# Decay tables of a long convolution: low factors from ScalarE exponentials instead of GpSimd products, amplitude multiplied in by VectorE, and a new placement of the side work

## The chip, the cores and the metric

One core of a Trainium2 chip runs the whole program. Its engines are TensorE (PE, with PEld for its weight loads), VectorE (DVE), ScalarE (ACT), GpSimd (POOL), and SyncE (SP), which here only issues transfers. Each engine works through its own list of instructions in the order written, and waits on semaphores of the others. The metric is the device time of one execution in microseconds (us); lower is better.

## The reference, cut to what matters

```python
h = layernorm(x) * (1 + ca) + sa                 # x: 2048 x 640; sa..gb from silu(c) @ w_mod
P = exp(dt * (A_re + 1j*A_im) * l)               # 640 channels x 192 states x 2048 steps
K = einsum("dn,dnl,dn->dl", C, P, dt * B).real   # a 2048-step filter for each channel
x = x + ga * (causal_conv(h, K) + h * Dskip)     # by FFT in the reference
h = layernorm(x) * (1 + cb) + sb
x = x + gb * (((h @ w_gate) * (h @ w_up)) @ w_down)   # 640 -> 1536 -> 640
```

## The kernel before, in words

The channels are taken in 5 blocks of 128 (`db`). Each block makes 8 groups (`n`, 40 in all), and each half block of 4 groups (`hf` = 0 to 9) has its own set of small tables. A group needs for its share of (channel, state) rows a decay `exp(a*l)` and a phase. The 2048 steps are split in two factors of a product, so that a matrix product over the states (`kg_ma`, `kg_mb`) gives the filter: `P` holds 32 values and `Q` 64 values a row, and both are a magnitude (`EP`, `EQ`) times a cosine or sine.

The magnitudes are outer products made by GpSimd in `outer` (line 716): `EP` from a low table `LP` (8 steps of 64) and a high table in `RH`; `EQ` from a low table `LQ` (8 consecutive steps, with the amplitude of the state in it) and a high table in `RH`. The phases `Ph` are integer outer sums of `LH` and `DH`, made on the same line. For every group GpSimd issues one `Ph`, one `EQ` and one `EP`. ScalarE then takes sines (`trig`), VectorE multiplies them with `EP` and `EQ` into `PtA`, `PtB`, `QtA`, `QtB` (lines 771, 772, 777, 797), and TensorE multiplies those.

The small tables of a block come from `u_seeds(db)`, a generator that is advanced a segment at a time; a letter string (`SEG`) says which steps (`s_l`, `s_a`, ...) a segment holds. Its core is a run on ScalarE of square root, exponentials (`s_e`), arctangent, with a load of a function table between kinds; after it the phase start `psi` goes through TensorE and VectorE to GpSimd (`weighted`). Before, `s_e` makes for each half the seven nontrivial columns of `LP` by seven exponentials of 96 elements, exponentiates `RH`, and exponentiates `RL`, three powers that `tab_eq` on GpSimd doubles into `LQ`: a copy of the amplitude, a product, and two doublings. `tab_ph` on GpSimd makes `LH` from `DL`, of which there are two buffers, one for each half; VectorE fills `DL` and `DH` in `s_d`.

The order around this is written out by a table. The main loop has 144 steps `t`, three to a group, and 24 more after the last group. At each step two calls of `due` issue the side jobs that fall into it. `SCHED` gives for each job the moment of each of its segments, 20 units to a step `t`, so 2400 is the end of the 40 groups; negative numbers fall into the prologue. The side jobs are the layernorm statistics (`st`, `hm`, `rstd`), the modulation rows (`ml`, `mr`, `mc`, `fo`), the seeds of the next block (`q`), the low tables (`low`), and the stages of the convolution: `pre` (first transform of h), `g`, `k` (transform of the filter), `c` (product and back), `d` (last stage and residual). The letters in `SLOT` give the ring buffer that each allocation takes. After the loop the gated product (the rest of the program) runs with an order of its own.

Of the kernel before, what the change touches and what calls it, by code (L numbers as in the profile page):

```python
# [31 lines left out]
    ml=(-885, -929, -989),  # L32
    mr=(((98, 154), (90, 130)), ((-884, 78), (-877, 73)), ((-885, -881), (-889, 132))),
    st=(
        (-955, 11),
        (-929, 195),
        (-874, 149),
        (-925, 128),
        (-938, 121),
        (-879, 152),  # L40
        (-869, 167),
        (-924, 162),
        (-995, -925),
        (-938, -871),
        (-885, 93),
        (-990, -871),
        (50, 180),
        (51, 214),
        (-930, -878),
        (-927, 39),  # L50
    ),
    hm=(
        (120, 388),
        (119, 390),
        (123, 234),
        (-949, 306),
        (-1000, 254),
        (112, 246),
        (231, 293),
        (-871, 309),  # L60
        (266, 333),
        (324, 384),
        (315, 372),
        (134, 256),
        (463, 511),
        (335, 429),
        (391, 541),
        (479, 545),
    ),
    rstd=(228, 229),  # L70
    tab=(487, 829),
    fo=(157, 189, 197, 222),
    e0=(138,),
    ds=(250, 255, 397, 411),
    mc=((-872, 289, 307, 356, 356), (217, 378, 439, 446, 461), (309, 570, 620)),
    q=(
# [4 lines left out]
    ),  # L81
    pre=(
# [5 lines left out]
    ),  # L88
    c=(
# [5 lines left out]
    ),  # L95
    d=(
# [5 lines left out]
    ),  # L102
    k=(
        (189, 202),
        (208, 226),
        (356, 358),
        (499, 559),
        (422, 496),
        (634, 660),
        (663, 672),  # L110
        (698, 713),
        (672, 682),
        (820, 837),
        (947, 972),
        (1036, 1059),
        (915, 955),
        (956, 984),
        (1080, 1094),
        (1072, 1079),
        (1271, 1275),  # L120
        (1209, 1209),
        (1528, 1540),
        (1546, 1546),
        (1406, 1429),
        (1384, 1393),
        (1533, 1569),
        (1521, 1521),
        (1684, 1715),
        (1706, 1716),
        (1931, 1933),  # L130
        (1939, 1951),
        (1911, 1915),
        (2069, 2083),
        (2033, 2056),
        (1997, 2004),
        (2286, 2306),
        (2108, 2128),
        (2368, 2376),
        (2349, 2373),
        (2504, 2534),  # L140
        (2413, 2437),
        (2492, 2495),
        (2495, 2507),
    ),
    low=((145, 411, 641, 885, 1122, 1398, 1592, 1847, 2073), (209, 434, 680, 929, 1150, 1398, 1612, 1868, 2112)),
    w=(2508, 2575, 2790, 2776, 2819, 2829),
    wl=(2444, 2450),
    wm=(2801, 2834),
    h=(2480, 2716, 2875, 2876, 2878, 2878, 2878, 2878),
    g=(  # L150
# [1716 lines left out]
```

## Time and profile before

| what | value |
|---|---|
| time, median of 3 runs | 983.3 us (982.86 to 986.79) |
| span of the profiled execution | 985.5 us |
| PE busy in it | 892.4 us (91%) |
| DVE busy | 717.3 us (73%) |
| ACT busy | 579.4 us (59%) |
| POOL busy | 513.1 us (52%) |
| last `EP` on POOL begins | 435.6 us |

The profile gives one execution, whose span from the first to the last instruction is 985.5 us; a time of its own beside that span is not shown, and the runs lie between 982.86 and 986.79 us. The shares of busy time are means over two stages that have little in common: until about 437 us GpSimd makes tables for the 40 groups and all engines share work, after about 531 us the gated product runs with TensorE nearly always busy, and between them lies the tail of the convolution. So the profile is read by stage.

### The profile page before, as it was taken

The numbers are of one execution on the slowest core, as the hardware profiler recorded it, in microseconds if no ns is written. First come the engines' busy times: TensorE is split into PE (matmuls) and PEld (weight loads), VectorE is DVE, ScalarE is ACT, GpSimd is POOL, SyncE is SP. The second block draws the span as 40 slices with busy tenths as digits, with TensorE's granted clock in tenths as the row PEclk, the third lists the DMA queues.
The fourth block names the chain that finished last, engine by engine and source line by source line (L and its number), as shares of the span: only waits on it lengthen the run. The fifth ranks groups of instructions, "written<-read, shape, count | busy, mean of one in ns | idle before, by whom it ended". The sixth has DMA issues, their size and how long they took to land.

```text
span 985.5 us, 26662 instructions
## 1 busy us (share of the span) xinstructions
PE 892.4 (91%) x11134; PEld 725.6 (74%) x11134; DVE 717.3 (73%) x1297; ACT 579.4 (59%) x1076; POOL 513.1 (52%) x400
## 2 busy tenths in 40 slices
PE   4767898899789888999879999999999999999998
PEld 3565656686476667677636888889999788888997
DVE  8798569888978888794867755557676656578952
ACT  4869989986878797873336433334455443435430
POOL 5988899799779979970030254440113132322110
PEclk9977789899989889999999999999999999999999
DMA  7746664555255434658695666733564576758875
GB/s 260 257 151 212 213 198 137 175 174 173 77 154 175 146 114 116 192 166 269 208 257 189 230 202 188 240 110 132 176 224 129 192 234 220 233 168 293 243 239 187
DMA packets 158816, 188.53 MB, mean 191 GB/s; under 512 B 9828, under 2 KB 128360, under 8 KB 157544
## 3 DMA queue, kind: packets, MB, share of 16 engines
q1 hardware_dynamic: 149480, 155.51, 49.1%
q0 software_dynamic: 4752, 21.63, 7.6%
q10 hardware_dynamic: 4464, 9.70, 2.6%
q8 instruction: 87, 1.43, 0.6%
q14 instruction: 33, 0.27, 0.1%
HBM read 124.22 MB, written 62.59 MB: 190 GB/s over the span
## 4 chain that ended last, share of the span: by engine, by line
PE 56%; ACT 14%; DVE 13%; issue 10%; POOL 4%; DMA 3%; SPq 0%; POOLq 0%; ACTq 0%; DVEq 0%
PE pa L1078 18%; PE psg L1078 9%; PE pa L1502 7%; PE kg L812 2%; PE kg L827 2%; PE psfc L894 2%; PE psfb L894 2%; PE psfc L950 2%; ACT trb L230 2%; ACT L230 2%; PE psfa L894 1%; ACT tra L230 1%; DVE QtA L772 1%; DVE QtA L771 1%; PE psfc L873 1%
## 5 line engine op out<-in xcount | busy, mean ns | idle before, releaser
L1055 POOL TENSOR_TENSOR tf<-wur,wgb 128x256 f32<-128x256 f32 x23 | 17.4, 755 | 243.0 <-DVE wtl L1026 196.5
L716 POOL TENSOR_TENSOR EQ<-LQ,RH 128x1536 f32<-128x1536 f32 x40 | 124.2, 3106 | 8.3 <-DVE QtB L772 8.1
L1026 DVE TENSOR_TENSOR wtl<-tf,wth 128x256 fp32r<-128x256 f32 (+1 forms) x72 | 37.3, 520 | 58.6 <-ACT wth L230 58.4
L716 POOL TENSOR_TENSOR Phb<-LH,DH 128x1536 int32<-128x1536 int32 x20 | 62.3, 3114 | 13.2 <-ACT tra L230 13.2
L716 POOL TENSOR_TENSOR EP<-LP,RH 128x768 f32<-128x768 f32 x40 | 66.1, 1653 | 0.0
L716 POOL TENSOR_TENSOR Pha<-LH,DH 128x1536 int32<-128x1536 int32 (+1 forms) x21 | 62.5, 2974 | 1.9 <-ACT trb L230 1.6
L1502 PE MATMUL pa<-wsg,sh 128*128 128x384 f32 (+1 forms) x304 | 57.3, 307 | 0.0
L827 PE MATMUL kg<-QtB,PtB 64*32 64x64 f32 x2560 | 49.3, 232 | 7.1 <-DVE QtB L772 7.1
L827 PEld LDWEIGHTS kg<-QtB,PtB 64*32 64x32 f32 x2560 | 42.8, 117 | 17.1 <-DVE QtB L772 8.5
L1541 POOL DMA_DIRECT2D wsg<-wdc x21 | 11.1, 531 | 66.5 <-PE pa L1554 35.5
L1502 PEld LDWEIGHTS pa<-wsg,sh 128*128 128x128 f32 x304 | 45.1, 188 | 0.0
L1026 DVE TENSOR_TENSOR wsg<-wga,wsg 128x640 fp32r<-128x640 f32 x36 | 33.8, 946 | 13.2 <-ACT wsg L230 13.2
L230 ACT ACTIVATE sh<-a 128x512 fp32r<-128x512 f32 x55 | 33.3, 624 | 13.9 <-PE psg L1554 6.2
L1026 DVE TENSOR_TENSOR sl<-a,sh 128x512 fp32r<-128x512 f32 x55 | 38.0, 710 | 3.9 <-ACT sh L230 3.9
L230 ACT ACTIVATE wsg<-wga 128x640 fp32r<-128x640 f32 x36 | 26.1, 730 | 24.8 <-PE pa L1502 12.1
L1078 PE MATMUL pa<-hh,wsg 128*128 128x512 f32 x150 | 39.9, 392 | 0.0
L771 DVE TENSOR_TENSOR QtA<-tra,EQ 128x1024 f32<-128x1024 f32 x20 | 24.4, 1221 | 18.1 <-PE kg L812 8.7
L1148 POOL TENSOR_SCALAR hfa<-xb,hr,hr 128x128 f32<-128x128 f32 x4 | 2.3, 577 | 67.0 <-DVE hr L285 67.0
L230 ACT ACTIVATE s<-pa 128x512 f32<-128x512 f32 x12 | 7.2, 599 | 49.1 <-PE pa L1078 49.1
L230 ACT ACTIVATE a<-pa 128x512 f32<-128x512 f32 x12 | 7.2, 597 | 48.4 <-PE pa L1078 48.4
L230 ACT ACTIVATE wth<-tf 128x256 fp32r<-128x256 f32 (+1 forms) x72 | 32.5, 482 | 4.6 <-DVE tf L1056 1.8
L1078 PE MATMUL pa<-sh,wth 128*128 128x512 f32 x110 | 34.0, 390 | 0.4 <-ACT a L230 0.4
(640 smaller groups left out, 3125.4 us busy)
## 6 DMA issues: line engine op xcount, KB each, us to landing
wsg<-wdc POOLq DMA_DIRECT2D x21, 640.0 KB, 4.8
wgb<-B_w_gate SPq DMA_DIRECT2D x24, 320.0 KB, 4.7
wur<-B_w_up SPq DMA_DIRECT2D x24, 320.0 KB, 5.7
wsd<-wsg SPq DMA_DIRECT2D x12, 640.0 KB, 4.2
wga<-wdg SPq DMA_DIRECT2D x12, 640.0 KB, 4.0
wsg<-wsd POOLq DMA_DIRECT2D x12, 640.0 KB, 4.9
wdc<-xb SPq DMA_DIRECT2D x21, 320.0 KB, 3.4
TVb<-WD SPq DMA_DIRECT2D x22, 256.0 KB, 3.4
```

The lines of the kernel that those rows point to most:

```text
L230: return S.activation(o, i, f, **kw)
L716: G.tensor_tensor(o.rearrange("p x (h l) -> p x h l", l=8), lo.unsqueeze(2).to_broadcast([P, rows, nh, 8]), hi.rearrange("p h x -> p x h") ...
L771: return [lambda: V.tensor_tensor(Qt[:, :, :, 0:32], tr[:, :, :, ::-1], e[:, :, 0:32].unsqueeze(1).to_broadcast([P, 2, R, 32]), op=OP.mult ...
L812: PE.matmul(kg[j * 32 : j * 32 + 32, dd, :], PtA[:, c, dl * 4 + j, :], QtA[:, c, dl * 4 + j, :], start=dd == 0 and c == 0, stop=False, til ...
L827: PE.matmul(kg[j * 32 : j * 32 + 32, dd, :], PtB[lo : lo + 64, c, r, :], QtB[lo : lo + 64, c, r, :], start=False, stop=dd == 7 and c == 1, ...
L894: PE.matmul(r[c][par * 64 : par * 64 + 64, i, :], t_tw[:, k0 + k, c, :], src[:, k, :], start=True, stop=True, tile_position=(0, par * 64))
L950: PE.matmul(r[par][:, i], t_ti[lo : lo + 64, qd * 4 + i, c, :], x[lo : lo + 64, c, i, :], start=c == 0, stop=c == 1, tile_position=(lo, 0))
L1026: V.tensor_tensor(lo, v, hi, op=OP.subtract)
L1055: E.tensor_tensor(t[:, 0:2], u[:, 0:2], g[:, 0:2], op=OP.subtract)
L1078: PE.matmul(ps, w[a][:, k], x[b][:, l], start=first and n == 0 and m == 0, stop=n == 2 and m == len(ks) - 1, skip_group_check=True)
L1502: PE.matmul(AC[tb][t][c], x[:, ts], w[:, cs], start=st, stop=f == NF - 1 and n == 2 and (c == 0 or t % 2 == 1))
L1541: G.dma_start(WD[q], wdc[:, q // 3, q % 3])
```

## The change

The low decay tables of the `Q` factor are no longer built by GpSimd. `s_e` issues two exponentials of 768 elements for each half, one for `LQ` and one for `LP`, both from the same eight rows of `RH` before `RH` itself is exponentiated. `RL` and `tab_eq` are gone. The amplitude is multiplied into the finished `LQ` by VectorE in `s_amp`, and `LQ` has three buffers. `DL` has one buffer instead of two; the second half of it is filled by a new step `s_D`, which comes as the last segment of the seeds, after `s_v`. A shift by zero replaces a cast, from a shift table with a twelfth entry. `weighted` runs once for a block, on both halves. For the last block, three of the four `g` tiles come from the ring `gh` instead of a large `f16` tile. All moments in `SCHED` and nearly all ring letters are new.

```diff
-    rstd=(228, 229),
-    e0=(138,),
+    rstd=(185, 108),
+    e0=(3, 0),
...
-    low=((145, 411, 641, 885, 1122, 1398, 1592, 1847, 2073), (209, 434, 680, 929, 1150, 1398, 1612, 1868, 2112)),
+    low=(161, 422, 658, 912, 1143, 1389, 1616, 1877, 2065),
...
-SEG = ("l", "a", "b", "c", "ud", "D", "r", "R", "x", "eE", "f", "g", "h", "v")
+SEG = ("l", "a", "b", "c", "ud", "r", "R", "x", "eE", "f", "g", "h", "v", "D")
...
+        def s_D():
+            free(1, "lh", "ph")
+            z = shl[:, 11:12].unsqueeze(2).to_broadcast([P, 4, 24])
+            st = bank("pd")[:, 0].bitcast(I32).rearrange("p (s r) -> p s r", r=24)[:, hs[1]]
+            V.tensor_tensor(st, sti[:, hs[1]], z, op=OP.logical_shift_left)
+            V.tensor_tensor(g5(DL)[:, 0, :, 0, :], t64[:, hs[1]], z, op=OP.logical_shift_left)
+            steps_of(1, st)
...
-            V.tensor_tensor(g4(Rl[h])[:, 0:3], ps[:, 0, hs[h]].unsqueeze(1).to_broadcast([P, 3, 4, 24]),
-                            mults[:, 11:14].unsqueeze(2).unsqueeze(3).to_broadcast([P, 3, 4, 24]), op=OP.mult)
...
         def s_e(h):
-            for l in range(1, 8):
-                act(Lp[h][:, :, l : l + 1], Rl[h][:, 0].unsqueeze(2), AF.Exp, scale=64.0 * l)
+            for t, m in ((Lq[h], 0.125), (Lp[h], 8.0)):
+                act(t.rearrange("p r l -> p l r"), Rh[h][:, 3:11], AF.Exp, scale=m)
             act(Rh[h], Rh[h], AF.Exp)
-            act(Rl[h][:, 0:3], Rl[h][:, 0:3], AF.Exp)
             mark("lp", 2 * db + h)
+
+        def s_amp(h, amp_):
+            need(1, "lp", 2 * db + h)
+            q4 = Lq[h].rearrange("p (s r) l -> p s r l", r=24)
+            V.tensor_tensor(q4, q4, amp_.unsqueeze(3).to_broadcast([P, 4, 24, 8]), op=OP.mult)
+            mark("lq", 2 * db + h)
...
-                G.tensor_tensor(t64[:, hs[h]], t64[:, hs[h]], st, op=OP.subtract)
-                G.tensor_tensor(s0, t64[:, hs[h]], psi[:, hs[h]], op=OP.add)
...
+                G.tensor_tensor(t64, t64, sti, op=OP.subtract)
+                for h, o in ((0, g5(DL)[:, 0, :, 0, :]), (1, t64[:, hs[1]])):
+                    G.tensor_tensor(o, t64[:, hs[h]], psi[:, hs[h]], op=OP.add)
...
-    def tab_eq(hf):
...
-        G.tensor_copy(LQ[:, :, 0:1], rl[:, 3].unsqueeze(2))
-        G.tensor_tensor(LQ[:, :, 1:2], rl[:, 3].unsqueeze(2), rl[:, 0].unsqueeze(2), op=OP.mult)
-        double(LQ, (rl[:, 1], rl[:, 2]), OP.mult)
```

On GpSimd, at the start of half 3 (the second half of block 1), this stands before: the group before ends with `EP`, then come the five instructions of `tab_ph`, the first `Ph` of the half, the four of `tab_eq`, and the first `EQ`. The digits behind a name tell the buffer.

```order
L716 TENSOR_TENSOR EP1_145<-LP2_149,RH2_156 128x768
L699 TENSOR_TENSOR DH0_159<-DH0_159 128x192
L700 TENSOR_TENSOR LH_150<-DL1_163,eighth_93 128x192
L701 TENSOR_TENSOR LH_150<-LH_150,DL1_163 128x192
L680 TENSOR_TENSOR LH_150<-LH_150,DL1_163 128x192x2
L680 TENSOR_TENSOR LH_150<-LH_150,DL1_163 128x192x4
L716 TENSOR_TENSOR Pha_1961<-LH_150,DH0_159 128x1536
L710 COPY LQ_146<-RL1_158 128x96
L711 TENSOR_TENSOR LQ_146<-RL1_158 128x96
L680 TENSOR_TENSOR LQ_146<-LQ_146,RL1_158 128x96x2
L680 TENSOR_TENSOR LQ_146<-LQ_146,RL1_158 128x96x4
L716 TENSOR_TENSOR EQ0_142<-LQ_146,RH0_154 128x1536
```

The same place on GpSimd after the change (line 716 is now 726, 699 to 701 are 719 to 721):

```order
L726 TENSOR_TENSOR EP1_143<-LP2_149,RH2_153 128x768
L719 TENSOR_TENSOR DH0_154<-DH0_154 128x192
L720 TENSOR_TENSOR LH_150<-DL_157,eighth_91 128x192
L721 TENSOR_TENSOR LH_150<-LH_150,DL_157 128x192
L700 TENSOR_TENSOR LH_150<-LH_150,DL_157 128x192x2
L700 TENSOR_TENSOR LH_150<-LH_150,DL_157 128x192x4
L726 TENSOR_TENSOR Pha_1904<-LH_150,DH0_154 128x1536
L726 TENSOR_TENSOR EQ0_140<-LQ0_144,RH0_151 128x1536
```

The four instructions of `tab_eq` are gone, `EQ` reads an `LQ` that has buffers of its own, and `tab_ph` reads the one `DL`.

On VectorE, at the end of the seeds of block 1 before, the arctangent's argument is made, the amplitudes are copied into the two `RL`, `psi` is written (line 651), and the products of the next group follow:

```order
L622 RECIPROCAL psfc_1143<-psfc_1143 128x192
L623 SCALAR_TENSOR_TENSOR pta_359<-pta_359,psfc_1143 128x192
L624 TENSOR_TENSOR psfc_1143<-pta_359,psfc_1143 128x192
L625 TENSOR_SCALAR pta_359<-psfc_1143 128x192
L650 COPY RL0_157<-psfb_1180 128x96
L650 COPY RL1_158<-psfb_1180 128x96
L651 TENSOR_SCALAR ptb_358<-psfb_1180 128x192
L771 TENSOR_TENSOR QtA_1219<-trb_1222,EQ0_142 128x32x32
L772 TENSOR_TENSOR QtA_1219<-trb_1222,EQ0_142 128x32x32
```

After the change, from `psi` on (line 663; 628 is the amplitude, 600 to 582 are `s_D`):

```order
L663 TENSOR_SCALAR ptb_534<-psfc_1194 128x192
L628 TENSOR_TENSOR LQ2_146<-LQ2_146,psfc_1194 128x768
L628 TENSOR_TENSOR LQ0_144<-LQ0_144,psfc_1194 128x768
L787 TENSOR_TENSOR PtAa_1168<-tra_1235,EP0_142 128x1024
L807 TENSOR_TENSOR PtB_1250<-trb_1252,EP0_142 128x512
L781 TENSOR_TENSOR QtB_1251<-trb_1252,EQ0_140 128x16x32
L782 TENSOR_TENSOR QtB_1251<-trb_1252,EQ0_140 128x16x32
L600 TENSOR_TENSOR psfa_1341<-pta_535,shl_78 128x96
L601 TENSOR_TENSOR DL_157<-ptb_534,shl_78 128x4x24
L579 TENSOR_TENSOR DL_157<-psfa_1341,shl_78 128x4x24
L582 TENSOR_TENSOR DL_157<-psfa_1341,shl_78 128x12x24
L582 TENSOR_TENSOR DH0_154<-psfa_1341,shl_78 128x8x24
```

Two products of 768 elements stand behind `psi`, and the filling of `DL` for the second half comes after them, where it needs `tab_ph` of the first half to be done on GpSimd.

On ScalarE, in the prologue before, the arctangent is followed by a copy of a modulation row, which TensorE must have made, and then by the first sines; the exponentials of the second half come later, in the third group:

```order
L230 ACT_TABLE_LOAD
L230 ACTIVATE pta_171<-pta_171 128x192
L230 ACTIVATE TVa_137<-psfa_313 1x384
L230 ACTIVATE ab_383<-Pha_249 128x512
L230 ACT_TABLE_LOAD
L230 ACTIVATE trb_382<-Pha_249 128x512
L230 ACTIVATE trb_382<-ab_383 128x512
L230 ACTIVATE ab_396<-Pha_249 128x512
```

After the change the copy is gone from this place, and the exponentials of the second half stand between the first and the second pair of sines:

```order
L235 ACTIVATE pta_165<-pta_165 128x192
L235 ACTIVATE ab_300<-Pha_248 128x512
L235 ACT_TABLE_LOAD
L235 ACTIVATE trb_299<-Pha_248 128x512
L235 ACTIVATE trb_299<-ab_300 128x512
L235 ACT_TABLE_LOAD
L235 ACTIVATE LQ1_145<-RH1_152 128x8x96
L235 ACTIVATE LP1_148<-RH1_152 128x8x96
L235 ACTIVATE RH1_152<-RH1_152 128x1056
L235 ACTIVATE ab_367<-Pha_248 128x512
L235 ACT_TABLE_LOAD
L235 ACTIVATE tra_366<-Pha_248 128x512
```

More of the change, by code (lines that the diff above doesn't have):

```diff
@@ new lines @@
+    d=(
[5 rows of a table added]
+    ),
+    k=(
+        (268, 332),
+        (352, 360),
+        (497, 513),
+        (457, 496),
+        (612, 626),
+        (628, 628),
+        (676, 691),
+        (742, 772),
+        (787, 824),
+        (864, 871),
+        (1053, 1074),
+        (1047, 1067),
+        (924, 928),
+        (936, 955),
+        (1090, 1094),
+        (1106, 1127),
+        (1249, 1277),
+        (1346, 1359),
+        (1517, 1522),
+        (1440, 1462),
+        (1449, 1463),
+        (1414, 1427),
+        (1564, 1568),
+        (1547, 1565),
+        (1782, 1793),
+        (1693, 1712),
+        (1887, 1911),
+        (2046, 2051),
+        (1874, 1910),
+        (1924, 1941),
+        (2010, 2010),
+        (2048, 2053),
+        (2287, 2321),
+        (2210, 2211),
+        (2322, 2327),
+        (2344, 2367),
+        (2461, 2508),
+        (2443, 2486),
+        (2516, 2531),
+        (2487, 2525),
+    ),
@@ L541, in free @@
                     need(1, k_, 4 * (hf - 3) + 3)
[L542 to L543 removed]
+                elif k_ == "lh" and hf:
+                    need(1, k_, hf - 1)
         def s_l():
@@ L634, in s_G @@
             if db == 0:
-                for h in range(2):
-                    act(g4(Rl[h])[:, 3], T["ps2"][:, 0, hs[h]])
+                act(keep_, T["ps2"][:, 0, hs[1]])
+                s_amp(0, T["ps2"][:, 0, hs[0]])
         def s_g():
@@ L1279, in tile_kernel @@
     at(T0["fo"], u_fold)
-    at(T0["e0"], once(lambda: LATE.pop()()))
+    for j in range(2):
+        at(T0["e0"][j : j + 1], once(lambda j=j: LATE[j]()))
     for j in range(4):
@@ L1295, in tile_kernel @@
         at(T0["k"][n], u_k, n)
-    for i, f in enumerate((tab_ph, tab_eq)):
-        for hf in range(1, 2 * NB):
-            at(T0["low"][i][hf - 1 : hf], once(f), hf)
+    for hf in range(1, 2 * NB):
+        at(T0["low"][hf - 1 : hf], once(tab_ph), hf)
     man = ctx.enter_context(ExitStack())
@@ L1324, in tile_kernel @@
             mod_i()
-    tab_eq(0)
     tab_ph(0, 0)
```

239 lines of the change are left out of this document (98 added, 141 removed), and 47 rows, old and new, of tables (c, d, g, pre).

## The prediction

> **What bounds the kernel now.** I read first the busy times by stage: the five blocks of table making (cut near where GpSimd starts a block's `tab_ph`), the tail, the gated product. The columns are length, busy time of each engine with its count, granted clock, DMA share, GB/s.
>
> ```profile
> 25.10:105.00 79.90, 58.20 (x907) 44.84 (x906) 64.21 (x137) 67.67 (x123) 68.16 (x42) 0.79 0.56 195
> 105.00:189.00 84.00, 75.41 (x1566) 50.52 (x1564) 67.25 (x98) 76.33 (x141) 77.52 (x45) 0.89 0.62 197
> 189.00:278.00 89.00, 79.51 (x1772) 59.32 (x1770) 75.06 (x109) 72.58 (x136) 76.81 (x49) 0.95 0.42 127
> 278.00:361.00 83.00, 69.70 (x1616) 54.18 (x1618) 69.65 (x102) 67.69 (x127) 75.39 (x45) 0.87 0.51 154
> 361.00:437.30 76.30, 69.99 (x1778) 53.34 (x1772) 63.91 (x79) 60.00 (x106) 75.40 (x45) 0.98 0.54 159
> 437.30:531.10 93.80, 79.28 (x1096) 57.79 (x1094) 61.08 (x148) 38.64 (x70) 9.36 (x15) 0.98 0.77 242
> 531.10:985.50 454.40, 449.09 (x2381) 397.69 (x2379) 294.78 (x540) 184.47 (x354) 116.87 (x138) 1.00 0.62 200
> ```
>
> From 25.1 to 437.3 GpSimd is the fullest engine: its five entries sum to 373.3 of 412.2 us, 90.6%. TensorE has 352.8 (86%), ScalarE 344.3 (84%), VectorE 340.1 (83%). After 531 TensorE has 449.1 of 454.4 us; nothing there is changed but which loads and splits are already done. So the change can act on the first 437 us and, by its placement, on the tail.
>
> Fullest is not yet bound. The chain that ended last says how much of it lay on GpSimd, and the list of waits who held whom:
>
> ```profile
> PE 56%; ACT 14%; DVE 13%; issue 10%; POOL 4%; DMA 3%; SPq 0%; POOLq 0%; ACTq 0%; DVEq 0%
> POOL Phb L716 <- ACT tra L230: 13.2, 4, 6.7
> POOL DL L656 <- issue: 10.6, 2, 7.9
> POOL EQ L716 <- DVE QtB L772: 8.1, 3, 5.0
> DVE QtA L771 <- POOL EQ L716: 1.6, 2, 1.2
> ```
>
> The first line is the whole program's chain; the others give total wait, times, longest. GpSimd waits 13.2 and 8.1 us for a buffer that ScalarE or VectorE still reads, and 10.6 us for `psi`; the others wait for GpSimd only 1 or 2 us here and there. A chain with 4% on the fullest engine means that four in-order engines pace each other. GpSimd works without pause for long, then stops once a block:
>
> ```profile
> 179.86 3.11 POOL L716 TENSOR_TENSOR Phb<-LH,DH 128x1536 int32<-128x1536 int32 x1 [4.65 <-ACT tra L230]
> 277.18 0.39 POOL L656 TENSOR_TENSOR DL<-ptb 128x96 int32<-128x96 int32 x1 [7.91 <-issue]
> ```
>
> The bracket is the idle time ahead. Such stops are the seeds of the next block, when ScalarE loads four function tables. At two places behind such a stop the chain does run through the work that is removed; this is the first (start, length, engine, tile, line), and the second is alike from 361 to 368:
>
> ```profile
> 102.61 0.38 POOL DL L656
> ...
> 106.70 1.57 POOL LH L680
> 108.28 0.30 POOL LQ L710
> 108.58 0.27 POOL LQ L711
> 108.92 0.57 POOL LQ L680
> 109.55 0.88 POOL LQ L680
> 110.43 3.12 POOL Pha L716
> ```
>
> **The change part by part.** GpSimd first, with the rows of `tab_eq`, of `weighted`, and of an integer operation 192 wide:
>
> ```profile
> L680 POOL TENSOR_TENSOR LQ<-LQ,RL 128x384 f32<-128x384 f32 x10 | 8.8, 879 | 0.8
> L680 POOL TENSOR_TENSOR LQ<-LQ,RL 128x192 f32<-128x192 f32 x10 | 5.6, 560 | 0.8
> L710 POOL COPY LQ<-RL 128x96 f32<-128x96 f32 x10 | 3.6, 358 | 0.0
> L711 POOL TENSOR_TENSOR LQ<-RL 128x96 f32<-128x96 f32 x10 | 3.9, 394 | 0.0
> L655 POOL TENSOR_TENSOR ptb<-ptb,DL 128x96 int32<-128x96 int32 x10 | 3.9, 386 | 0.3 <-DVE ptb L589 0.3
> L699 POOL TENSOR_TENSOR DH<-DH 128x192 int32<-128x192 int32 x9 | 5.4, 597 | 0.0
> ```
>
> `tab_eq` costs 8.8 + 5.6 + 3.6 + 3.9 = 21.9 us, 2.19 a half. In `weighted`, ten subtractions (3.9) become five of double width at 0.597 (3.0): 0.9 less. That is 22.8 us; 2.2 of it lie in the prologue, 20.6 in the blocks.
>
> The prologue I set to zero. Before, ScalarE stands 9.3 us behind a modulation row that TensorE makes, so that the first product on VectorE starts at 30.45; the change takes the row away, but puts the second half's exponentials and a table load there, and VectorE's first product now stands behind the amplitude of that half. The exponentials leave 43.9 to 49.2, where they stood before.
>
> ```profile
> 26.82 0.48 ACT L230 ACTIVATE TVa<-psfa 1x384 f32<-1x384 f32 x1 [9.34 <-PE psfa L363]
> 30.45 1.22 DVE L771 TENSOR_TENSOR QtA<-trb,EQ 128x1024 f32<-128x1024 f32 x1 [4.67 <-ACT trb L230]
> 43.90 1.28 ACT L230 ACT_TABLE_LOAD   x1
> 12.74 1.43 ACT L230 ACTIVATE LP<-RL 128x96 f32<-128x96 f32 x7
> L230 ACT ACTIVATE RH<-RH 128x1056 f32<-128x1056 f32 x10 | 10.8, 1084 | 0.0
> L230 ACT ACTIVATE RL<-RL 128x288 f32<-128x288 f32 x10 | 4.2, 424 | 0.0
> ```
>
> ScalarE's exponentials: no row has 768 elements written eight apart. On the line between 288 elements (424 ns) and 1056 (1084 ns) 768 take 0.84 us. The upper bound is the seven strided columns, 672 elements in 1.43 us, which gives 1.63. I take 0.84, since those seven also pay seven starts. A half then has 2 x 0.84 for 1.43 + 0.42, 0.2 us less, or 1.4 more at the bound; over the eight halves of blocks 1 to 4, where this run lies ahead of `psi` and so on the path, that is 1.4 us gained or 11 lost. Besides, the two square roots of the statistics come apart (`rstd` 185 and 108), and the order of the changed kernel has 25 table loads for 23, two more at 1.28 us. They fall in the first block, where GpSimd has 11.7 us of idle time; I charge them nothing, and 2.6 if that cover is gone. On the load itself "ScalarE: Activation LUTs" of the Trainium skill, section "What ACT_TABLE_LOAD costs", adds a drain and reckons 2.66 us for a switch, by which the two would cost 5.3. The rows here show 1.28 from one instruction to the next, and the sum goes by them.
>
> VectorE's new work is bracketed by its own products:
>
> ```profile
> L771 DVE TENSOR_TENSOR QtA<-trb,EQ 128x1024 f32<-128x1024 f32 x20 | 24.4, 1221 | 13.2 <-ACT trb L230 8.5 <-issue 1.8 <-ACT tra L230 1.4
> L797 DVE TENSOR_TENSOR PtB<-trb,EP 128x512 f32<-128x512 f32 x20 | 13.7, 686 | 14.5 <-ACT trb L230 11.8 <-PE psfc L873 2.7
> L595 DVE TENSOR_TENSOR RL<-psfa,mults x4: 448/448/448, 88.9 to 346.4; 128x288 f32<-128x288 f32 x4
> L650 DVE COPY RL<-psfb x4: 247/252/258, 101.8 to 276.5; 128x96 f32<-128x96 f32 x4
> ```
>
> The amplitude, 768 elements, lies halfway between 0.69 and 1.22: 0.95, ten times 9.5. Gone are ten products for `RL` (4.5) and eight copies (2.0). `s_D` adds two operations of 96 (0.25 each) a block, 2.5, and a second copy of the step, 192 wide, makes 1.7 (0.35 each, between 0.25 for 96 and 0.45 for 288). The casts into `DL` become shifts of the same size. VectorE gains 7.2 us of work. The amplitudes stand behind `psi`, so GpSimd goes from `weighted` to the end of `tab_ph` while VectorE does them; on the chain above that took from 102.61 to 108.27, 5.7 us, and a pair of `weighted` less makes it 5.3. So 1.9 us lie beside 5.3. What follows them on VectorE, the next products, is later by 1.9 - 0.5 = 1.4 us a block; I charge a quarter of it, 0.35 x 4 = 1.4, since VectorE is idle 17% of the time there.
>
> **Placement** moves every side job but keeps the design: the third block's `c`, for one, ends at 2393 for 2412, and before 2400 about the same jobs are done. In the tail (437 to 531) the last `c` ends at 2689 for 2801, the last `d` at 2872 for 2879; TensorE is busy 79.3 of 93.8 us there, so at most 14.5 are open. I put it at zero, from -4 to +4. The three `g` tiles that move to the ring `gh` are loads well ahead of use, also nothing.
>
> How much of the 20.6 us counts? The low end is the chain's two places, 2 x 2.19 = 4.4. The high end is all 20.6, if GpSimd stays 90.6% busy. Between them lie seven of nine tables, off the chain; time freed there turns at first into a longer stop of GpSimd at the block's end, and counts only as far as the new placement lets the other three close up. They stand at 83 to 86% and would have to rise to 87 to 91. I take half of the 16.2 us, because neither end is excluded: 8.1. Sum: 4.4 + 8.1 + 1.4 (exponentials) - 1.4 (amplitude) = 12.5 us, from which I take off 1.5 for table loads and stray waits: 11 us. The span of 985.5 becomes 974.5; the median of the runs is 2.2 us below that span, and 983.3 becomes 972.
>
> **The rivals.**
>
> *All of it counts.* GpSimd sets the pace throughout and the new placement keeps it as full: 983.3 - 20.6 = 963. For it speaks the even fullness of the other engines, against it the 4% on the chain. TensorE's clock could help: it is 0.79 and 0.87 in the first and fourth block, and a group's `kg` products take 1.86 us on the chain at 184 against 1.03 at 214:
>
> ```profile
> 184.23 1.86 PE kg L827 x64
> 214.20 1.03 PE kg L827 x64
> ```
>
> "TensorE: Matmul & The Clock Gate" (Trainium skill, "What's actually happening") has the clock fall to half after an idle window of about 3.4 us and rise after as long a busy one. The two rows agree, 1.8 to 1. With the clock at 1.00 in the first and fourth block their 127.9 us of TensorE would shrink by about 21 us, of which only what is waited for would show; it is a reason to leave the range open downward.
>
> *Nothing but the chain's places.* Consumers set the pace, GpSimd only waits longer: 983.3 - 4.4 = 979, within 0.5% of before. That speed is what the waits by themselves suggest.
>
> *Slower, by the single `DL`.* VectorE may not fill `DL` for the second half before GpSimd has done `tab_ph` of the first, and waits in order, with the next group's products queued behind it and ScalarE and TensorE behind those. In block 1 `s_D` is at 428 and that `tab_ph` at 422: between `psi` and `s_D` VectorE has two amplitudes, one product of 1024 and three of 512, 1.9 + 1.2 + 2.1 = 5.2 us, for GpSimd's 5.3, so it waits next to nothing, but 3.1 us more for each full outer product (`Phb` above) that GpSimd still has ahead. In the other blocks the distance is 96, 38 and 143 units, two steps or more. It takes over 4 us in each of four blocks to pass the bound; at 5, or 20 us, the time is 983.3 - 11 + 20 = 992.
>
> **How the numbers follow.** A difference of 0.5% (4.9 us) is about what a measurement of this kernel can tell from none. Part of it counts (966 to 977, forecast 972): 0.45. All of it (under 966): 0.20. Nothing but the chain's places (977 to 988): 0.22. Slower (over 988): 0.13. Faster takes the first two and a little of the third: 0.66; the same 0.21; slower 0.13. The range of 958 to 986 leaves out the slower case and some 0.05 of the second; it holds the exponentials at their upper bound (972 + 11 + 1.4 = 984).
>
> **What the changed profile would show.**
>
> ```profile
> L716 POOL TENSOR_TENSOR EP<-LP,RH x40: 1635/1652/1682, 15.8 to 435.6; 128x768 f32<-128x768 f32 x40
> ```
>
> Right: the last `EP` on GpSimd begins near 425 us instead of 435.6, and the gated product starts as much earlier; exponentials of 768 near 0.84 us and amplitudes near 0.95; GpSimd's stops at the blocks' ends grow, but by less than 4 us each. The prediction fails if the last `EP` stays at 435 (consumers), if VectorE waits at `s_D` for `LH` by several us a block (slower), or if the tail takes other than 90 to 98 us, since then the placement and not the tables decides.

## The result and the profile after

The changed kernel takes 997.5 us (median of 4 runs, 996.43 to 998.86), beside 983.9 us for the kernel before (982.86 to 986.79). The ratio is 1.0138, 95% interval 1.0111 to 1.0166: slower by 13.6 us, where 11 us of gain were forecast. The profiled execution of the changed kernel took 996.86 us, with a span of 995.1 us. The profile of the kernel before has a span of 985.5 us, 9.6 less, so the stages compared below account for 9.6 of the 13.6 us. In the other runs a time is some 1.8 us above its own span, so that profile was of a longer execution than the median.

The busy times by stage of the changed kernel, cut at the same events as before (the columns are again length, PE, PEld, DVE, ACT, POOL with counts, granted clock, DMA share, GB/s). The last two rows are the tail and the gated product:

```profile
26.60:112.00 85.40, 60.92 (x985) 44.94 (x987) 72.52 (x136) 69.01 (x104) 65.43 (x31) 0.82 0.67 230
112.00:198.80 86.80, 70.68 (x1484) 46.94 (x1478) 68.52 (x97) 74.92 (x122) 74.47 (x40) 0.89 0.46 144
198.80:293.00 94.20, 81.08 (x1768) 61.25 (x1766) 76.40 (x109) 76.64 (x127) 71.96 (x37) 0.92 0.44 129
293.00:382.00 89.00, 76.51 (x1710) 55.98 (x1712) 77.17 (x110) 73.68 (x120) 71.91 (x37) 0.91 0.53 155
382.00:453.80 71.80, 63.83 (x1649) 50.01 (x1638) 65.14 (x80) 56.48 (x100) 71.23 (x36) 0.98 0.53 158
453.80:541.00 87.20, 78.70 (x1158) 58.50 (x1155) 63.60 (x152) 41.62 (x75) 8.90 (x16) 1.00 0.80 253
541.00:995.10 454.10, 447.87 (x2376) 396.54 (x2374) 293.15 (x537) 183.08 (x351) 116.04 (x138) 1.00 0.62 199
```

The five blocks take 427.2 us for 412.2: 15.0 us more. The tail takes 87.2 for 93.8, 6.6 less, the gated product takes the same 454 us, and the blocks begin 1.5 us later (26.6 for 25.1). In the blocks GpSimd's work did shrink, from 373.3 to 355.0 us, yet so did its share: 355.0 of 427.2 is 83.1%, for 90.6% before. It worked less and waited more. The chain that ended last, the waits of GpSimd in the blocks (total, times, longest) and its last `EP` say for whom:

```profile
PE 54%; ACT 19%; DVE 10%; issue 9%; DMA 5%; POOL 2%; SPq 0%; ACTq 0%; DVEq 0%; POOLq 0%
POOL Phb L726 <- ACT tra L235: 27.9, 5, 12.4
POOL DL L668 <- issue: 16.4, 2, 12.2
POOL EQ L726 <- DVE QtB L782: 14.2, 8, 3.6
POOL Pha L726 <- ACT trb L235: 7.8, 2, 4.1
L726 POOL TENSOR_TENSOR EP<-LP,RH x40: 1635/1650/1691, 17.9 to 452.2; 128x768 f32<-128x768 f32 x40
```

ScalarE's share of the chain rose from 14 to 19%. The four waits sum to 66.3 us, for 13.2 + 10.6 + 8.1 + 1.6 (the last for `Pha`) = 33.5 before. The stop at the end of each of the first four blocks grew: 2.65 to 4.27 us, 4.65 to 9.15, 7.91 to 12.17 and 6.75 to 12.39. The last `EP` begins at 452.2 instead of 435.6; the forecast was 425.

What ScalarE does at a seed run shows why. This is the run of the last block, in the timeline of the kernel before and then of the changed one (start, length, instruction):

```profile
344.88 1.43 ACT L230 ACTIVATE LP<-RL 128x96 f32<-128x96 f32 x7
346.10 1.08 ACT L230 ACTIVATE RH<-RH 128x1056 f32<-128x1056 f32 x1
347.09 0.42 ACT L230 ACTIVATE RL<-RL 128x288 f32<-128x288 f32 x1
347.42 1.41 ACT L230 ACTIVATE LP<-RL 128x96 f32<-128x96 f32 x7
```

```profile
358.58 1.62 ACT L235 ACTIVATE LQ<-RH 128x768 f32<-128x768 f32 x1
359.99 1.62 ACT L235 ACTIVATE LP<-RH 128x768 f32<-128x768 f32 x1
361.64 1.08 ACT L235 ACTIVATE RH<-RH 128x1056 f32<-128x1056 f32 x1
362.63 1.60 ACT L235 ACTIVATE LQ<-RH 128x768 f32<-128x768 f32 x1
```

One half took 347.42 - 344.88 = 2.54 us and now takes 362.63 - 358.58 = 4.05 us. The exponentials of 768 take 1.60 us, not 0.84. The chain that ended last runs through this whole run, from 355.39 to 365.68.

The other cost is on VectorE. It is busy 738.2 us for 717.3, where 7.2 more were forecast. In the groups of VectorE (total, mean in ns) and in a stretch of its timeline, set beside GpSimd's for the same time, small operations last for microseconds:

```profile
L600 DVE TENSOR_TENSOR psfc<-pta,shl 128x96 int32<-128x96 int32 x2 | 5.1, 2568 | 0.0
L601 DVE TENSOR_TENSOR DL<-ptb,shl 128x96 int32<-128x96 int32 x5 | 4.1, 827 | 0.0
L287 DVE TENSOR_TENSOR ry<-ry,rv 128x6 f32<-128x6 f32 x1 | 3.0, 3009 | 0.0
L287 DVE TENSOR_TENSOR ry<-ry,rv 128x10 f32<-128x10 f32 x1 | 0.2, 169 | 0.0
```

```profile
306.49 2.96 DVE L600 TENSOR_TENSOR psfc<-pta,shl 128x96 int32<-128x96 int32 x1
309.37 0.25 DVE L601 TENSOR_TENSOR DL<-ptb,shl 128x96 int32<-128x96 int32 x1
64.88 3.01 DVE L287 TENSOR_TENSOR ry<-ry,rv 128x6 f32<-128x6 f32 x1
```

```profile
306.22 3.11 POOL L726 TENSOR_TENSOR Phb<-LH,DH 128x1536 int32<-128x1536 int32 x1
64.79 3.08 POOL L726 TENSOR_TENSOR EQ<-LQ,RH 128x1536 f32<-128x1536 f32 x1
```

An operation of one size takes 0.25 us or 2.96, 0.17 or 3.01, and each long one ends when GpSimd's outer product ends: 306.49 + 2.96 = 309.45, for 306.22 + 3.11 = 309.33; 64.88 + 3.01 = 67.89, for 64.79 + 3.08 = 67.87. All of them read SBUF only; the copy of line 600 writes to PSUM (`psfc`), the others to SBUF. The profile shows the wait as busy time, and no list of waits has it. Over the blocks this is about 8 us in the two copies of `s_D` and 8 us in the row statistics. The chain that ended last runs through all the long operations of the statistics (start, length on the chain); of the copies it has one long one, 2.88 us at 306.57:

```profile
46.57 2.42 DVE rv L283
62.94 1.92 DVE ry L286
64.88 3.02 DVE ry L287
67.92 1.59 DVE ry L288
```

### The profile page after: what moved, and what is told of

The parts are those of the page before. It is cut to its first block, busy times and chain, and to the rows that moved or that the text cites. A ratio compares the mean times of both kernels' runs of the same rounds, so it can differ in the third digit from the quotient of the medians.

```text
span 995.1 us, 26550 instructions
## 1 busy us (share of the span) xinstructions
PE 890.2 (89%) x11134; PEld 722.1 (73%) x11134; DVE 738.2 (74%) x1299; ACT 595.5 (60%) x1017; POOL 492.2 (49%) x355
## 3 DMA queue, kind: packets, MB, share of 16 engines
q8 instruction: 87, 1.43, 0.6%
## 4 chain that ended last, share of the span: by engine, by line
PE 54%; ACT 19%; DVE 10%; issue 9%; DMA 5%; POOL 2%; SPq 0%; ACTq 0%; DVEq 0%; POOLq 0%
PE pa L1086 17%; PE psg L1086 8%; PE pa L1509 7%; ACT tra L235 3%; PE kg L822 2%; ACT trb L235 2%; PE psfa L904 2%; ACT L235 2%; PE psfc L904 1%; PE kg L837 1%; PE psfb L958 1%; PE psfb L859 1%; ACT LQ L235 1%; DMA wga<-B_w_gate 1%; ACT LP L235 1%
## 5 line engine op out<-in xcount | busy, mean ns | idle before, releaser
L837 PEld LDWEIGHTS kg<-QtB,PtB 64*32 64x32 f32 x2560 | 40.0, 111 | 15.0 <-issue 6.7
L837 PE MATMUL kg<-QtB,PtB 64*32 64x64 f32 x2560 | 46.5, 224 | 3.9 <-DVE QtB L782 3.1
L1086 PE MATMUL pa<-sl,wth 128*128 128x512 f32 x110 | 34.1, 391 | 0.0
```

The costliest lines, as they stand in the source:

```text
L837: PE.matmul(kg[j * 32 : j * 32 + 32, dd, :], PtB[lo : lo + 64, c, r, :], QtB[lo : lo + 64, c, r, :], start=False, stop=dd == 7 and c == 1, ...
L1086: PE.matmul(ps, w[a][:, k], x[b][:, l], start=first and n == 0 and m == 0, stop=n == 2 and m == len(ks) - 1, skip_group_check=True)
```

## The experiments

Theory A: the exponentials, longer than forecast, delay everything behind the seeds. Theory B: the new placement or the single `DL` costs the time. Theory C: VectorE's waits behind GpSimd cost it. Ratios are to the kernel before, with 95% intervals, from runs on the same chip. Differences in us are between medians. The kernel before had medians of 982.5 to 984.8 us beside these runs, so a difference between two runs is uncertain by a few us; where the ratios give another size, it is said.

**What GpSimd's tables were worth, and the new tables in the old order.** In the kernel before, the four table operations go, and `EQ` reads a table that is filled once:

```diff
 def tab_eq(hf):
...
-    G.tensor_copy(LQ[:, :, 0:1], rl[:, 3].unsqueeze(2))
-    G.tensor_tensor(LQ[:, :, 1:2], rl[:, 3].unsqueeze(2), rl[:, 0].unsqueeze(2), op=OP.mult)
-    double(LQ, (rl[:, 1], rl[:, 2]), OP.mult)
```

> The kernel before, with GpSimd's four table operations per half for the low amplitude table left out (the table is filled once and never rebuilt, so the output is not the reference's); everything else, order and side jobs included, as before. It measures what that GpSimd time is worth where it stood. The prediction's credit (4.4 us at two places of the chain plus half of the other 16.2 us) gives 983.9 - 12.5 = about 971 us. All of it counted: about 963. If GpSimd's consumers set the pace and its time is worth little: 980 to 984.

Measured: 981.58 us, ratio 0.9983 (0.9964 to 1.0002). GpSimd loses 20.2 us of work (513.1 to 492.9) and the kernel at most 3.5 us. The second run puts the new tables into the old `SCHED` with two `DL` buffers; GpSimd's products read a constant `LQ` (the edit is shortened):

```diff
 def s_e(h):
-    for l in range(1, 8):
-        act(Lp[h][:, :, l : l + 1], Rl[h][:, 0].unsqueeze(2), AF.Exp, scale=64.0 * l)
+    for t, m in ((Lx, 0.125), (Lp[h], 8.0)):
+        act(t.rearrange("p r l -> p l r"), Rh[h][:, 3:11], AF.Exp, scale=m)
     act(Rh[h], Rh[h], AF.Exp)
-    act(Rl[h][:, 0:3], Rl[h][:, 0:3], AF.Exp)
+ # s_v: Lx times the amplitude on VectorE; tab_eq gone
```

> The kernel before in its own order and with its two shift tables, with only the new tables put in: two exponentials of 768 per half written 8 apart, the amplitude multiplied in by VectorE, no table operations on GpSimd (the outer products read a constant low amplitude table because three buffers do not fit beside two shift tables; the output is not the reference's). Theory A, the tables themselves cost: exponentials at 1.60 us make the seed run some 1.2 us per half longer and GpSimd's saving is worth little, so 990 to 997 us. Theory B, the new placement and the single shift table cost: 972 to 984, and the changed kernel's 997.5 comes from the rest. The prediction's credit with the exponentials at their real length would be 983.9 - 12.5 + 11 + 2.9 = about 985.

Measured: 1002.04 us, 1.0183 (1.0157 to 1.0210), 20 us above the run without GpSimd's tables. So the loss comes with the tables themselves, without the new order and with two `DL`; theory B is not needed for it, though this doesn't exclude that it adds something. The changed kernel (1.0138) is, if anything, a little better than this; the intervals touch.

**VectorE behind GpSimd.** The zero of the two copies in `s_D` comes from PSUM:

```diff
 def s_D():
     free(1, "lh", "ph")
-    z = shl[:, 11:12].unsqueeze(2).to_broadcast([P, 4, 24])
-    st = bank("pd")[:, 0].bitcast(I32).rearrange("p (s r) -> p s r", r=24)[:, hs[1]]
+    pd = bank("pd").bitcast(I32)
+    V.memset(pd[:, 1, 0:1], 0)
+    z = pd[:, 1, 0:1].unsqueeze(2).to_broadcast([P, 4, 24])
+    st = pd[:, 0].rearrange("p (s r) -> p s r", r=24)[:, hs[1]]
```

> The changed kernel, with one small edit: the zero by which the late shift step copies two 128x96 blocks on VectorE comes from PSUM instead of SBUF, so that these two copies (up to 2.96 us each in the changed kernel's trace, while GpSimd runs) have one operand in SBUF instead of two. Theory C (VectorE waits for GpSimd's running instruction when both operands are in SBUF): the two copies fall to about 0.25 us everywhere; if VectorE's time there is on the path, 989 to 994 us, if it is covered, 996 to 998. If the long copies are something else (a wait that the profile counts as running), they stay at 1.7 to 3 us.

Measured: 993.07 us, 1.0097 (1.0073 to 1.0122), 4.4 us below the changed kernel, with intervals that overlap. The groups of VectorE in this run, the two copies and then an operation of the statistics, which was left as it was:

```profile
L602 DVE TENSOR_TENSOR psfc<-pta,psfc 128x96 int32<-128x96 int32 x2 | 0.5, 262 | 0.1
L603 DVE TENSOR_TENSOR DL<-ptb,psfc 128x96 int32<-128x96 int32 x2 | 0.5, 254 | 0.1
L283 DVE TENSOR_SCALAR rv<-mv 128x6 f32<-128x6 f32 x1 | 3.1, 3078 | 0.0
```

All ten copies are at 0.25 to 0.26 us; the untouched one still waits 3 us. The next run gives the statistics PSUM operands too, and the amplitude of half 1, which had taken 3.8 us in the run just told, for 0.97 in the changed kernel (the edit is shortened; the copies are as in that run):

```diff
 def row_stats(q0, q1):
-    rstd(mv1[:, s_, :], rs1[:, s_], nm1[:, s_], rv[:, s_], ry[:, s_])
+    pr = ps_f.tile([P, 2, 256], F32, name="psfc" if q0 == 0 else "psfa", bufs=1)
+    v, y, r = (pr[:, 0, 64 * i : 64 * i + q1 - q0] for i in range(3))
+    # the same steps, each with an operand in PSUM
 def s_E0():
     s_e(1)
-    s_amp(1, keep_)
+    act(kb, keep_)      # kb: 96 values in a PSUM bank
+    s_amp(1, kb)
```

> The changed kernel with every VectorE step that was seen waiting behind GpSimd given a PSUM operand: the two copies of the late shift step, the two row statistics steps (their small operands move to PSUM, one copy more each), and the amplitude product of half 1 (3.8 us in the trace of the run before; its amplitude is copied to PSUM by ScalarE first). Theory C: these steps fall by some 8 + 8 + 3 us of VectorE time; if half of that is on the path, 988 to 991 us; if all, 980 to 983; if none, 993 (as with the two copies alone) to 998.

Measured: 989.57 us, 1.0065 (1.0043 to 1.0087), 7.9 us below the changed kernel (7.2 by the ratios): about half of the time that VectorE had waited. Here every operation of the statistics is at 0.15 to 0.22 us:

```profile
L1275 DVE TENSOR_SCALAR psfc<-mv 128x6 f32<-128x6 f32 x1 | 0.2, 168 | 0.1
```

**The exponentials.** First I stored `LQ` and `LP` power by power, so that ScalarE writes side by side:

```diff
-    LQ = [pk1.tile([P, 96, 8], F32, name=f"LQ{i}") for i in range(3)]
+    LQ = [pk1.tile([P, 8, 96], F32, name=f"LQ{i}") for i in range(3)]
...
-    act(t.rearrange("p r l -> p l r"), Rh[h][:, 3:11], AF.Exp, scale=m)
+    act(t, Rh[h][:, 3:11], AF.Exp, scale=m)
```

> The changed kernel with both low decay tables stored power by power, so that ScalarE writes its 768 values side by side and VectorE multiplies them side by side; GpSimd's outer products read them 96 apart instead. Same values, same order. Theory A (the strided writes carry the loss): the exponentials fall from 1.60 to about 0.85 us, the seed run by about 1.4 us per half, time 984 to 989 us. Theory B (placement, or VectorE's waits behind GpSimd): 994 to 998. If GpSimd reads 96 apart more slowly, its outer products grow past 2.9 us and the time goes above 998.

Measured: 1008.18 us, 1.0252 (1.0233 to 1.0271), slower still. Groups of ScalarE and GpSimd in the blocks:

```profile
L235 ACT ACTIVATE LQ<-RH 128x768 f32<-128x768 f32 x8 | 6.7, 835 | 0.0
L726 POOL TENSOR_TENSOR EQ<-LQ,RH 128x1536 f32<-128x1536 f32 x37 | 149.5, 4041 | 6.8 <-DVE QtB L782 6.8
L726 POOL TENSOR_TENSOR EP<-LP,RH 128x768 f32<-128x768 f32 x36 | 75.6, 2100 | 0.0
```

The exponentials are as short as forecast, but GpSimd, which now reads the low table 96 apart, pays 0.92 us on each `EQ` and 0.45 on each `EP`, 55 us in all. So this run moved the cost to another engine and says nothing on theory A. The next leaves the low tables alone and stores `RH` row by row:

```diff
-    RH = [pk1.tile([P, 11, 96], F32, name=f"RH{i}") for i in range(3)]
+    RH = [pk1.tile([P, 96, 11], F32, name=f"RH{i}") for i in range(3)]
...
-    act(t.rearrange("p r l -> p l r"), Rh[h][:, 3:11], AF.Exp, scale=m)
+    act(t, Rh[h][:, :, 3:11], AF.Exp, scale=m)
```

> The changed kernel with the high decay table RH stored row by row (96 rows of 11) instead of power by power, so that both low decay tables are still stored as GpSimd reads them and ScalarE's two exponentials write 768 values side by side (they read runs of 8, 11 apart). Same values, same order. Theory A (the strided writes carry the loss): exponentials at about 0.85 us instead of 1.60, GpSimd's outer products unchanged at 3.1 and 1.65 us, time 985 to 990 us. Theory C (VectorE behind GpSimd) or the placement alone: 995 to 998 although the exponentials got short. If ScalarE pays for strided reads as it does for strided writes, the exponentials stay at 1.6 us and nothing changes.

Measured: 979.65 us, 0.9992 (0.9968 to 1.0015), 17.9 us below the changed kernel. Its ten runs lie between 977.28 and 987.22 us, three of them over 984, and the ratios make it 14.4 us. Then the same in the old order, on the run with the new tables and two `DL`:

> The run with the new tables in the old order and two shift tables (1002 us), with RH row by row, so that its exponentials write side by side; the outer products read a constant low amplitude table, the output is not the reference's. With the run without GpSimd's tables (981.6 us) as the floor: theory A gives 1002 - 12 = about 990, and what is left over 981.6 is VectorE's amplitude products. If the strided writes weren't it: 999 to 1003.

Measured: 988.31 us, 1.0060 (1.0036 to 1.0085), 13.7 us less (12.1 by the ratios). And with strided exponentials but without VectorE's amplitude:

```diff
 def s_amp(h, amp_):
-    V.tensor_tensor(q4, q4, amp_.unsqueeze(3).to_broadcast([P, 4, 24, 8]), op=OP.mult)
```

> The run with the new tables in the old order and two shift tables (1002 us, strided exponentials), with VectorE's amplitude products left out (the table keeps no amplitude; the outer products read a constant table anyway; the output is not the reference's). If the products (9 of 0.95 us after the psi step) are on the path: 992 to 995. If VectorE covers them: 1000 to 1004. Theory A expects the strided exponentials to keep at least 10 us above the 981.6 us floor: not under 990.

Measured: 997.58 us, 1.0158 (1.0120 to 1.0195), between the two expectations. It is 4.5 us below the run with amplitudes (2.5 by the ratios), but the intervals overlap: the amplitude costs between nothing and about 5 us. The one-line repair, to turn the stride from the write to the read, came next:

```diff
-    act(t.rearrange("p r l -> p l r"), Rh[h][:, 3:11], AF.Exp, scale=m)
+    act(t, Rh[h][:, 3:11].rearrange("p l r -> p r l"), AF.Exp, scale=m)
```

> The changed kernel with one line changed: each of the two exponentials writes its 768 values side by side and reads them 96 apart, instead of reading side by side and writing 8 apart. Tables, order and everything else as in the changed kernel. If only a strided write costs ScalarE time: exponentials about 0.85 us, time 978 to 984 us as with RH row by row. If a strided read costs the same: 1.6 us and 995 to 998.

Measured: 998.13 us, 1.0165 (1.0120 to 1.0209), no gain. ScalarE pays for a strided read nearly what it pays for a strided write:

```profile
L235 ACT ACTIVATE LQ<-RH 128x768 f32<-128x768 f32 x9 | 13.9, 1544 | 0.1
```

The row by row run had left a doubt. Its groups of ScalarE and GpSimd show that GpSimd got faster as well, since it reads the high table 1 apart instead of 96:

```profile
L235 ACT ACTIVATE LQ<-RH 128x768 f32<-128x768 f32 x8 | 6.8, 851 | 0.0
L726 POOL TENSOR_TENSOR EQ<-LQ,RH 128x1536 f32<-128x1536 f32 x40 | 115.4, 2885 | 13.6 <-DVE QtB L782 13.6
L726 POOL TENSOR_TENSOR EP<-LP,RH 128x768 f32<-128x768 f32 x39 | 60.2, 1545 | 0.0
```

Three runs part the two: only the exponentials short, the same in the old order, and only GpSimd's products short.

```diff
 # exponentials alone
-    act(t.rearrange("p r l -> p l r"), Rh[h][:, 3:11], AF.Exp, scale=m)
+    act(t.rearrange("p r l -> p (r l)"), Rh[h][:, 3:11].rearrange("p l r -> p (l r)"), AF.Exp, scale=m)
 # GpSimd alone: RH row by row, and
+    act(t.rearrange("p r l -> p l r"), Rh[h][:, :, 3:11].rearrange("p r l -> p l r"), AF.Exp, scale=m)
```

> The changed kernel, tables laid out as in it, with both exponentials reading and writing 768 values side by side; the values land in the wrong places of the table, so the output is not the reference's. Row by row storage had shortened two things at once: the exponentials (1.60 to 0.85 us, 20 of them) and GpSimd's outer products (3.12 to 2.88 and 1.65 to 1.55 us, 40 of each, 14 us in all). Here only the exponentials get short. If they carry the 18 us: about 980. If GpSimd's outer products carried half of it: 986 to 990. If all: 995 to 998.

> The same edit in the run with the new tables in the old order with two shift tables (1002 us): both exponentials read and write side by side with misplaced values, GpSimd's outer products as before (the output is not the reference's). If the exponentials carry the loss there: 987 to 990, as with rows (988.3). If GpSimd's faster outer products had carried half of that: about 995.

> The complement: the changed kernel with RH row by row, so that GpSimd's outer products are as short as there (2.88 and 1.55 us), but the exponentials still go through the table power by power (they read 11 apart and write 8 apart, about 1.6 us each). Same values. If the exponentials carry the 18 us: 994 to 998. If GpSimd carries half: about 989. If all: 980.

Measured: exponentials alone 984.91 us, 1.0020 (0.9999 to 1.0042), 12.6 us below the changed kernel (11.6 by the ratios); in the old order 987.21 us, 1.0043 (1.0023 to 1.0064), 14.8 below its strided twin (13.8 by the ratios); GpSimd's products alone 999.20 us, 1.0168 (1.0141 to 1.0195), no gain. The groups of the first and the last of the three:

```profile
L235 ACT ACTIVATE LQ<-RH 128x768 f32<-128x768 f32 x8 | 6.7, 835 | 0.0
L726 POOL TENSOR_TENSOR EQ<-LQ,RH 128x1536 f32<-128x1536 f32 x40 | 124.8, 3121 | 14.1 <-DVE QtB L782 14.0
```

```profile
L235 ACT ACTIVATE LQ<-RH 128x768 f32<-128x768 f32 x9 | 14.5, 1612 | 0.1
L726 POOL TENSOR_TENSOR EQ<-LQ,RH 128x1536 f32<-128x1536 f32 x38 | 109.7, 2887 | 18.5 <-DVE QtB L782 18.5
```

With short exponentials and GpSimd at its old 3.12 us nearly all of the loss is gone; with GpSimd at 2.89 us and long exponentials none of it. Theory A holds in both orders.

**The price of GpSimd's time in the new order, and both repairs together.** On the row by row kernel, 2.2 us of repeated integer table work per half (the edit is shortened):

```diff
+    def again(hf):
+        G.tensor_tensor(LH[..., 0:1], d[0], eighth_, op=OP.add)
+        G.tensor_tensor(LH[..., 1:2], LH[..., 0:1], d[1], op=OP.add)
+        G.tensor_tensor(LH[..., 2:4], LH[..., 0:2], d[2], op=OP.add)
...
+        at([T0["low"][hf - 1] + 25], once(again), hf)
```

> The changed kernel with RH row by row (979.7 us), plus three repeated GpSimd operations per half (0.55 + 0.69 + 0.94 us, the first steps of the integer table computed again with the same result), in the half's first unit: about the 2.2 us per half that the change took off GpSimd. It gives the price of that time in the new order. All of it on the path: 979.7 + 20 = about 999. The half that the prediction credited: about 990. Nothing, as in the old order (981.6 against 983.4): 978 to 983.

Measured: 991.86 us, 1.0089 (1.0060 to 1.0119): 12.2 us more (9.5 by the ratios) for 18.9 us of GpSimd time (busy 499.2 for 480.3). Last, `RH` row by row and the PSUM operands together:

> The changed kernel with both repairs: RH row by row (the exponentials write side by side, 997.5 to 979.7 us by itself) and PSUM operands for the VectorE steps that waited behind GpSimd (997.5 to 989.6 by itself). If the two costs are separate, as theories A and C say together: 979.7 - 7.9 = about 972 us, below both kernels by 1.1% of the kernel before. If they were the same time counted twice (the steps waited only because ScalarE's longer run had moved them under GpSimd's work): 978 to 981.

Measured: 970.36 us (966.69 to 971.65), 0.9856 (0.9831 to 0.9881). The sum of the two repairs gives 971.7 by the medians; by the ratios, the two together brought 27.7 us where singly they brought 14.4 and 7.2. Either way they do not overlap: theories A and C are two separate costs, and this version is faster than both kernels. Its chain has ScalarE back at 15%, and the four waits of GpSimd sum to 51.0 us, for 66.3 in the changed kernel:

```profile
PE 58%; ACT 15%; DVE 10%; issue 10%; DMA 4%; POOL 1%; SPq 0%; DVEq 0%; POOLq 0%; ACTq 0%
POOL Phb L730 <- ACT tra L235: 21.9, 5, 10.5
POOL Pha L730 <- ACT trb L235: 10.6, 2, 6.1
POOL DL L670 <- issue: 10.6, 2, 9.4
POOL EQ L730 <- DVE QtB L786: 7.9, 7, 2.6
```

## Why the prediction failed, point by point

**GpSimd's saving** was right as work: 20.9 us less (513.1 to 492.2) for 22.8. Its worth was not. The credit was the chain's two places and half of the rest, 12.5 us; taken off in the old order it brought 1.8 us, at most 3.5. The step that failed is "I take half of the 16.2 us, because neither end is excluded", and the two places of the chain too: with that work gone, GpSimd's four waits grew from 33.5 to 43.8 us. The rival "nothing but the chain's places" was the nearest of the four in this step. The price is no constant: about 2 us a half cost 9.5 to 12.2 us for 18.9 when put back on the row by row kernel, and GpSimd's shorter outer products brought nothing beside long exponentials (999.2 for 997.5) and perhaps 3 to 5 us beside short ones (979.65 for 984.91, intervals that overlap). That fits the reading that GpSimd's time counts where nobody else is later.

**The exponentials** are the largest single error. The step chose 0.84 us "since those seven also pay seven starts" over the row's 1.63; the trace has 1.60. That row was the only one with the new write pattern, and it had the price almost exactly: 1.43 us for 672 elements and 1.60 for 768 are both 2.1 ns an element, so the seven starts added next to nothing. With 0.84 us (the run with the exponentials alone) the changed kernel takes 984.9 instead of 997.5: 12.6 us (11.6 by the ratios), for the 11 + 1.4 that the prediction kept as the far end. The bound was in the range, but only as a mishap to an otherwise sound gain.

**VectorE's new work** was counted well by instruction (amplitudes 0.95 forecast, 0.942 to 0.971 measured; the copies of `s_D` 0.25 forecast, 0.25 to 0.26 in the run where they don't wait) and missed by what is not an instruction's own: some 16 us of waiting behind GpSimd, a term that the sum doesn't have, and 7.9 us of time. The two copies of `s_D` have two inputs in SBUF and now stand in the middle of GpSimd's outer products; the row statistics, moved to 108 and 185, do too. The trace of before had one warning, which the prediction does not use. In the timeline of VectorE and of GpSimd there:

```profile
68.34 1.41 DVE L278 TENSOR_SCALAR rv<-mv 128x6 f32<-128x6 f32 x1
71.14 0.17 DVE L278 TENSOR_SCALAR rv<-mv 128x10 f32<-128x10 f32 x1
```

```profile
66.61 3.11 POOL L716 TENSOR_TENSOR Phb<-LH,DH 128x1536 int32<-128x1536 int32 x1
74.70 3.10 POOL L716 TENSOR_TENSOR EQ<-LQ,RH 128x1536 f32<-128x1536 f32 x1 [4.97 <-DVE QtB L772]
```

The first of the statistics' operations lasts until 69.75, when `Phb` ends (69.72); all the others fell into the 4.97 us in which GpSimd stood idle, and took 0.17 to 0.22. A row eight times as long as its twin was the thing to ask about before moving the statistics elsewhere. The charge of 1.4 us for the amplitude lies in the 0 to 5 us that the run without it leaves.

**The rival "slower by the single `DL`"** had the right sign and the wrong mechanism. VectorE never waited for `LH` there by the list of waits; the single `DL` cost time through the copies that it made necessary. Its 992 us came from 5 us a block that don't exist.

**Placement, tail and table loads.** Set at zero from -4 to +4, the tail moved by -6.6 us, to 87.2, outside the 90 to 98 that the prediction named as a sign of failing. Its work did not shrink (TensorE 78.7 us for 79.3, VectorE 63.6 for 61.1), so idle time fell; whether by the new moments is not shown, and it was a gain, so it isn't what failed. The other signs failed too: the last `EP` came 16.6 us later, and three of GpSimd's four stops at the blocks' ends grew by more than 4 us. The prologue, set to zero, ends 1.5 us later (26.6 for 25.1). Table loads are 26 for 24 over the program, two more as counted. They were charged nothing, but beside the two square roots of the statistics the chain now has two loads (1.28 us each, at 50.18 and 61.17) where it had one (at 73.31); no run prices this. The new tables take 1.0183 in the old order and 1.0138 in the new one, so the new order as a whole is no cause of the loss, though its moments for the statistics brought their waits.

In sum, the forecast missed by 25.5 us: 12.6 for the exponentials, 7.9 for VectorE's waits, each by its own run. By the ratios these two are 11.6 and 7.2. The remaining 5 to 7 us fit the overrated GpSimd time, which in the old order was worth some 10 us less than credited, against the tail's gain; no run splits that rest, and its cause stays open.

## What to carry to other kernels

Where the only row with a new access pattern is long, take that row's rate per element and not one from side by side data; then lay out the tables so that every reader and writer finds its elements side by side, asking it for every engine that touches them (one layout here saved 0.77 us on ScalarE and cost 0.92 on GpSimd, the other saved on both). Before moving small VectorE work under a busy GpSimd, look whether all that it reads is in SBUF; one input in PSUM was enough to free the operations with two. And time taken off the fullest engine need not be worth anything by itself: remove the work in a trial run first. Here that run showed 1.8 us, and it could have been made before anything was built on 12.5.

## What the runs showed of the hardware

ScalarE's exponential of 128x768 takes 0.83 us side by side, 0.85 reading runs of 8 that are 11 apart, 1.54 reading 96 apart, 1.60 writing 8 apart (four bytes a value), and 1.61 with both a strided read and a strided write. "Advanced Engine Details and Errata" of the Trainium skill, section "SBUF Cachelines", has lines of 16 bytes and a penalty when each access falls into another line, with two hits a line enough to hide it; the five figures agree with that, runs of 8 included.

GpSimd's outer product of 1536 takes 2.88 us with the high table 1 apart, 3.12 with it 96 apart, and 4.04 with the low table, which is read innermost, 96 apart as well.

Small VectorE operations that read SBUF only, even of 6 values a partition, last until the running GpSimd instruction ends, up to 3.08 us for 0.17, and the profile counts it as busy time. This is shown for copies, products and scalar steps. An output in PSUM did not free the copy of line 600, which has two inputs in SBUF (2.96 us). With one input in PSUM none of the copies and products waited (0.25 to 0.26 us and 0.17 to 0.18), nor did the one-input step of the statistics that then wrote to PSUM (0.17 us at 61.72, in a GpSimd instruction from 61.50 to 64.60). Not every operation waits: in the changed kernel a `BATCH_NORM_AGGREGATE` took its usual 0.21 us at 43.03, within a GpSimd instruction from 41.19 to 44.28, and a reciprocal 0.19 us at 62.71, within one from 61.71 to 64.83. GpSimd can be the one that waits: beside VectorE's product of two SBUF tables (26.52 to 27.49) an `EQ` took 3.81 us, for a median of 3.10. "SBUF — State Buffer" of the Trainium skill, section "SBUF: two separate sides", names a pair of ports that the two engines lock for a whole instruction, VectorE when it has two SBUF inputs or runs in a two-port mode; the ends of the pairs above agree to 0.12 us.
